# Moving scale matmuls, casts and weight loads around the start of the first token mixer (one core)

## The chip, the cores and the metric

The kernel runs on one core of a Trainium2 chip. The metric is device time in microseconds (us) of one execution; lower is better. TensorE (PE in the profile) multiplies, VectorE (DVE), ScalarE (ACT) and GpSimd (POOL) work element by element, and SyncE (SP) and GpSimd issue the transfers between HBM and the on-chip memory. Every engine runs its own instructions in order and waits for others by semaphores.

## The reference

Four layers in a row on one array x of 2048 tokens by 640 channels: a spectral layer, a token mixer, the spectral layer again, the token mixer again. Each starts from a layer norm and adds its result to x.

```python
def _A_ref(x, w_r, w_i):                      # spectral: 2-D FFT, times a filter, back
    X = jnp.fft.rfft2(x, axes=(-2, -1)) * (w_r + 1j * w_i)
    return jnp.fft.irfft2(X, s=(S, D), axes=(-2, -1))

def _B_ref(x, w1, b1, w2, b2):                # mixer over the tokens
    h = _layernorm(x, axis=-1)                                  # (B, S, D)
    u = _gelu(jnp.einsum("bsd,sf->bdf", h, w1) + b1)            # (B, D, F), F = 1728
    y = jnp.einsum("bdf,fs->bds", u, w2) + b2
    return y.transpose(0, 2, 1)

x = x + _A_ref(_layernorm(x, axis=-1), A_w_r, A_w_i)
x = x + _B_ref(_layernorm(x, axis=-1), B_w1, B_b1, B_w2, B_b2)
x = x + _A_ref(_layernorm(x, axis=-1), A_w_r, A_w_i)
x = x + _B_ref(_layernorm(x, axis=-1), B_w1, B_b1, B_w2, B_b2)
```

## The kernel before, in words

**Rows and tiles.** The 2048 tokens are 16 rows (j = 0 to 15) of 128 tokens; F is 14 tiles of 128. All products are made of float16 pairs: a value is a high part (`hi`, a cast on ScalarE) and a low part (`lo`, the rest, on VectorE), and `mm3` adds high x high, high x low and low x high in PSUM.

**Order.** While `self.pin` is set, every instruction issued through `V`, `G`, `T` or `PE` keeps its place in the program's order *on its own engine* (an edge to the instruction before it on that engine). Everything else, DMA issues among it, is placed by a planner: as soon as its operands and its buffer are free in the planner's own estimate of time, the earlier one in the program first. `with self.after(x):` puts an edge of issue order between `x` and those instructions of the block that stand on the engine of `x`.

**The stages around the change.** The first spectral layer ends in `a2(0)`, a software pipeline over the rows: step i makes the last inverse products of row i (`id_mm`), of row i - 1 (`is1_mm`), adds the result of row i - 2 to x, takes the mean and variance of row i - 3, and normalizes row i - 4 or i - 5. For that a power on GpSimd gives the factor `r`, GpSimd gives the bias `nb`, and ScalarE writes the normalized row `hf[k]`. Rows 0 to 7 get their high part `hha` right there. Between the rows stand pieces of the first weight tiles: `wload(m)` issues the two 512 KB loads `raw` of weight tile m, `scan1(m)` sums its squares on ScalarE (written to `junk`), `wsplit(m)` makes the pair `wh`, `wl` of it.

`b1st` is the first token mixer. At its start ScalarE casts rows 8 to 15 to `hhb`; `hlow(c)` makes the low parts on VectorE (`hl` for rows 0 to 7, c = 0 and 1; `hlb` for rows 8 to 15, c = 2 and 3). `prod` then multiplies them with weight tiles 0 and 1 (rows 0 to 11 first: `early`, rows 12 to 15 after: `late`), `both` with tiles 2 and 3. `keep5` forms sums of raw tiles for later use (`X`, on GpSimd) and stores them.

**Scales.** Each weight tile, or pair of tiles, has a power-of-two scale from the sum of its squares. `scale1` is a generator in three steps: the first `next` adds the sums on VectorE (`sqb`), the second is one TensorE matmul with ones (`ps<-sqb,ones`) that adds over the partitions, the third reads it on VectorE and makes the scale. `step(m)` is one `next`.

**The 35 products.** F tiles 0 to 4 and 7 to 11 are done by the seven-product scheme of Strassen and Winograd, `ops`, n = 0 to 34: `product(n)` is 24 matmuls on TensorE (eight j of `mm3`), `work(n)` the rest: `evict(n - 1)` of the PSUM result, `hi(n + 3)` and `lo(n + 3)` of a coming weight, and what `todo[n]` lists. `mms` says after which n the matmul of a scale stands:

```python
        mms = {7 * d - 6: 2 * d + PAIR for d in range(1, 5)}     # n = 1, 8, 15, 22
        mms.update({27: a, 33: b})
...
        for n in range(len(ops)):
            product(n)
            work(n, todo[n])
            if n in mms:
                step(mms[n])
```

The first step of that scale is in `todo[n]`, the third in `todo[n + 1]`. After the 35 products come the 16 rows of the second product (the loop over j, 28 entries i of up to three matmuls each), which also starts the next spectral layer; it is not pinned up to j = 12. There the last two steps of the scale of tile m + 2 stand at i = 6 and 7.

The second mixer, `b2nd`, begins with the same casts of rows 8 to 15, but not pinned.

Of the kernel before, what the change touches and what calls it, by code (L numbers as in the profile page):

```python
# [15 lines left out]
AF = mybir.ActivationFunctionType  # L16
ALU = mybir.AluOpType
# [3 lines left out]
S, D, NL, F = 2048, 640, 321, 1728  # L21
NJ, NG, NFT = 16, 16, 14
# [32 lines left out]
PAIR = 4  # L55
# [35 lines left out]
class Layers:  # L91
# [697 lines left out]
    def a2(self, li):  # L789
        nc, A = self.nc, self.A  # L790
        first = li == 0
        V, G, T = self.V, self.G, self.T
# [11 lines left out]
        p = self.push("a2", side=self.sq)  # L804
# [50 lines left out]
        xt, pd, eo, p1, ec, mv, vs, rb = ({} for _ in range(8))  # L855
# [3 lines left out]
        for i in range(NJ + 5):  # L859
            has = [0 <= i - k < NJ for k in range(6)]  # L860
            if has[0]:
                pd[i] = id_mm(i)
            if has[1]:
                k = i - 1
                eh, ps = eo[k], pd.pop(k)
                el = elow(ps, eh)
                if not first and i == NJ:
                    self.pss0 = self.big()
                    for j in HA:
                        for a in range(2):  # L870
                            mm(self.pss0[:, a, :320], self.w[0][0][:, j], self.hh[j][:, a], start=j == 0, stop=False)
                p1[k] = is1_mm(eo.pop(k), el, tIM[k // 4][:, k % 4])
            if first and i == 10:
                next(sc)
            if has[4]:
                v, mean = vs.pop(i - 4)
                r = self.t(p, [128, 1], F32, "r", 3)
                G.tensor_tensor(r, v, self.mh, op=ALU.pow)
                b = self.t(p, [128, 1], F32, "nb", 3)
                G.tensor_scalar(b, mean, r, -1.0, op0=ALU.mult, op1=ALU.mult)  # L880
                rb[i - 4] = r, b
            if has[2]:
                k = i - 2
                x, ps = xt[k], p1.pop(k)
                o = ps[:, 1]
                e = self.t(p, [128, 324], F32, "ec", 2)
                T.activation(e[:, :322], ps[:, 0, :322], AF.Copy)
                V.tensor_tensor(v2(x, 160, NL), v2(x, 160, NL), v2(o, 161, 1), op=ALU.subtract)
                V.tensor_tensor(x[:, :NL], x[:, :NL], o[:, :NL], op=ALU.add)
                if first and i == 11:  # L890
                    next(sc)
                G.tensor_tensor(v2(x, 160, NL), v2(x, 160, NL), v2(e, 161, 1), op=ALU.add)
                G.tensor_tensor(x[:, :NL], x[:, :NL], e[:, :NL], op=ALU.add)
            for k in (i - 4,) if not first or i >= NJ else (i - 5,) if i < NJ - 1 else (i - 5, i - 4):
                if not 0 <= k < NJ:
                    continue
                r, b = rb.pop(k)
                f = self.hf[k]
                T.activation(f, xt.pop(k)[:, :D].rearrange("p (a b) -> p a b", a=2), AF.Identity, scale=r, bias=b)
                if k in HA:  # L900
                    T.activation(self.hh[k], f, AF.Copy)
            k = i if first else i + 1
            if 2 <= k < NJ:
                xt[k] = xload(k)
            if has[2]:
                nc.sync.dma_start(self.xs[li + 1][i - 2], xt[i - 2][:, :D])
            if has[3]:
                st = self.stats1(p, xt[i - 3])
                m = self.stats2(p, st)
                v = self.t(p, [128, 1], F32, "v", 2)  # L910
                V.tensor_scalar(v, m[:, 1:2], (1.0 + EPS) / ZS ** 2, EPS * EPS / ZS ** 2, op0=ALU.mult, op1=ALU.add)
                vs[i - 3] = v, m[:, 0:1]
            if has[0]:
                eo[i] = ehigh(pd[i])
            if i in (1, 2):
                self.wsplit(0, (1,), hi=False, part=slice(i * 4 - 4, i * 4))
            if first and i in (4, 5):
                self.wsplit(0, (0,), hi=False, part=slice(i * 4 - 16, i * 4 - 12))
            if i == 3:
                self.wload(1)  # L920
                self.wopen(1)
            if first:
                if i in (6, 7):
                    self.scan1(1, (i - 6,))
                if i == 8:
                    sc = self.scale1(1, at=lambda: p1[i - 1][:, 1, 400:401])
                    next(sc)
            if i in (12, 13):
                self.wsplit(1, (i - 12,), lo=False)
            if first and i == 14:  # L930
                self.wsplit(1, (0,), hi=False)
            if first and i in (10, 13, 16):
                self.wload({10: 2, 13: 3, 16: 5}[i])
            if i in (1, 4, 8):
                mload()
        self.pin = False
# [116 lines left out]
    def b1st(self, li):  # L1053
        nc, A = self.nc, self.A
        V, G, T = self.V, self.G, self.T
# [6 lines left out]
        H = self.halves(ph, pt, hx)  # L1062
        prod, tsum, thi, tlo, hlow, hhigh, hlows = H.prod, H.tsum, H.thi, H.tlo, H.hlow, H.hhigh, H.hlows
        spot = [None]
        sc = {m: self.scale1(m, at=lambda m=m: spot[0][:, m % 4:m % 4 + 1]) for m in range(2, NFT + 2)}
        sc.update({m: self.scale1(m) for m in range(NFT + 2, NFT + NJ)})
        self.pin = True

        def step(m):
            if m in sc:  # L1070
                next(sc[m])
# [17 lines left out]
        def keep5(a):  # L1089
            ssum(5, a, G)  # L1090
            nc.gpsimd.dma_start(self.ws1[5][a], src(5, a))
# [19 lines left out]
        bank, f = {}, {}  # L1111

        def product(n):
            o = self.big()
            bank[n], spot[0] = o[:, 0, :320], o[:, 1, 0:4]
            for j in range(8):
                self.mm3(bank[n], (wo[n][:, 0, j], wo[n][:, 1, j]), H.operand(PB[ops[n][1]], j), j == 0, j == 7)

        def gelu(o, x=None, **q):
# [56 lines left out]
        upart = lambda ft, a, i: U[ft % 7][:, i, ft // 7 * 2 + a]  # L1176


        for j in range(8, NJ):
            T.activation(H.hhb[:, j - 8], self.hf[j], AF.Copy)  # L1180
        self.wsplit(1, (1,), hi=False)
        self.wload(PAIR)
        self.scan1(2)
        self.scan1(3)
        hlow(0)
# [10 lines left out]
        hlow(2)  # L1196
        step(2)
        step(3)
        keep5("S1")
        prod(pss[1], w1[0], hhigh, early, start=True)  # L1200
        step(3)
        self.scan1(4)
        self.scan1(5)
        hlow(3)
        step(3)
        step(4)
        for i, q in ((0, w0[0]), (0, w0[1]), (1, w1[0])):
# [56 lines left out]
        for d in range(1, 5):  # L1264
            a, b, n = 2 * d + PAIR, 2 * d + PAIR + 1, 7 * d
# [10 lines left out]
        a, b = NFT, NFT + 1  # L1276
# [10 lines left out]
        todo[32] += [lam(self.wopen, a), lam(self.wsplit, a, (0,))]  # L1287
        todo[33] += [lam(self.wsplit, a, (1,))]
        todo[34] += [lam(uhi, 4, 0, 2), lam(ulo, 4, 0, 2)]
        mms = {7 * d - 6: 2 * d + PAIR for d in range(1, 5)}  # L1290
        mms.update({27: a, 33: b})

        for e in todo[-5]:
            e()
        for j in every:
            if j % 4 == 0:
                work(j // 4 - 4, todo[j // 4 - 4])
            both(ps, w, j)
            if j % 4 == 3 and j // 4 - 4 in mms:
                step(mms[j // 4 - 4])  # L1300
        plain(3, f[5][:, 2:4], flat(ps))
        for n in range(len(ops)):
            if n == 3:
                self.pop("hf")
                pu = self.push("u", side=self.sp)
                U.update({e: pu.tile([128, 2, 4, 320], F16, name=f"u{e}_{self.n}") for e in range(7)})
            product(n)
            work(n, todo[n])
            if n in mms:
                step(mms[n])  # L1310
        evict(len(ops) - 1)
        evicted(len(ops) - 1)
        uhi(4, 2, 2)
# [11 lines left out]
        p = self.pT  # L1325
# [42 lines left out]
        for j in range(NJ):  # L1368
# [7 lines left out]
            xt = xts[j][:, :D]  # L1376
# [17 lines left out]
            for i, (ft, a) in enumerate(order):  # L1394
                if tail and i == NFT:
                    half(0)
                if j == NJ - 2 and i in (4, 20):
                    flush(1)
                if j >= NJ - 2 and i in (6, 12, 17):
                    next(row)  # L1400
                if tail and i == 2:
                    self.wopen(0)
                    self.wsplit(0, lo=False)
                if i in (4, 8):
                    next(steps, None)
                if j == NJ - 3 and i == 9:
                    self.wload(0)
                if i in (6, 7):
                    step(m + 2)
                if i in (15, 18):  # L1410
                    self.scan1(m + 3, (i // 3 - 5,))
                if i == 26 and m + 3 < NFT + NJ:
                    step(m + 3)
                o = pss[a][:, :320]
                if ft < NFT - 1:
                    self.mm3(o, (wh[:, ft], wl[:, ft]), (upart(ft, a, 0), upart(ft, a, 1)), ft == SEQ[0], ft == SEQ[-1])
                else:
                    mm(o, wh[:, ft], upart(ft, a, 1), start=False, stop=False)
                    mm(o, wl[:, ft], upart(ft, a, 0), start=False, stop=False)
# [722 lines left out]
```

## Time and profile before

| | |
|---|---|
| Time, median of 3 runs | 998.46 us (997.73 to 999.18) |
| The profiled execution | 1002.54 us; its span, first to last instruction, 1000.5 us |
| Mean granted TensorE clock over the span | 0.986 |
| PE busy | 942.2 us (94%), 9009 matmuls |
| DVE, ACT, POOL busy | 758.1 us (76%), 563.8 us (56%), 325.9 us (33%) |
| Moved by DMA | 176.28 MB, mean 176 GB/s |

All times below are us from the start of the span. In the profile's lines nearly all instructions have line 83, which is the helper that issues them, so they are told apart by the names of their tiles: `out<-in`. `a2(0)` lies at about 122 to 179, the start of `b1st` at 179 to 229, the 35 products at 237 to 360, the rows of the second product from there to about 555. The same places of the second half of the kernel lie at 622 to 678 and from there on. A row of the timeline gives start, duration, engine, instruction, tiles, count, and in brackets the idle time of the engine before it with what ended it. A row of the windows gives the stretch, its length, the busy time of PE, weight loads, DVE, ACT, POOL with counts, the granted clock (1.00 is full speed), the share of time in which the DMA engines were busy, and GB/s.

### The profile page before, as it was taken

What the parts mean: (1) busy time and instruction counts of PE and PEld (TensorE: products, weight loads), DVE (VectorE), ACT (ScalarE), POOL (GpSimd) and SP (SyncE); (2) the same over time, 40 slices, a digit from 0 to 9 for tenths busy, and PEclk for the clock granted to TensorE, in tenths of its full rate; (3) what the DMA queues carried; (4) which work ended last, traced back from release to release, by engine and by line L of the source; (5) the groups of instructions that cost most, each with busy time, mean ns of one, the idle gap of its engine ahead of it and who ended that gap; (6) DMA issues with size and microseconds to landing.
All of it is one profiled execution on the core that took longest, in us unless ns stands there. A gap on an engine that the chain in (4) does not pass through costs nothing.

```text
span 1000.5 us, 22481 instructions
## 1 busy us (share of the span) xinstructions
PE 942.2 (94%) x9009; PEld 697.2 (70%) x9009; DVE 758.1 (76%) x1392; ACT 563.8 (56%) x864; POOL 325.9 (33%) x515
## 2 busy tenths in 40 slices
PE   4889898699999989999999998999999999999998
PEld 3768776376677657777777687776777777777776
DVE  7989878879877866666666798789834455998885
ACT  5857768757656667555543377585533444454431
POOL 6949757551222322222222298573000000000000
PEclk9999999799999999999999999999999999999999
DMA  8866386345777675464321465475555447755411
GB/s 260 274 176 172 118 308 231 122 138 182 246 248 247 212 251 183 134 207 129 125 86 73 138 186 168 148 230 170 183 154 167 144 131 247 242 170 198 146 46 53
DMA packets 67244, 176.28 MB, mean 176 GB/s; under 512 B 7914, under 2 KB 15236, under 8 KB 67140
## 3 DMA queue, kind: packets, MB, share of 16 engines
q1 hardware_dynamic: 59380, 146.39, 46.6%
q0 software_dynamic: 7760, 28.46, 7.6%
q8 instruction: 70, 1.15, 0.5%
q14 instruction: 34, 0.28, 0.1%
HBM read 127.24 MB, written 47.58 MB: 175 GB/s over the span
## 4 chain that ended last, share of the span: by engine, by line
PE 50%; DVE 7%; ACT 3%; POOL 3%; issue 2%; DMA 2%; SPq 0%; DVEq 0%; ACTq 0%; POOLq 0%
PE ps L83 50%; DMA raw<-w2z 1%; DVE xt L83 1%; DVE u L83 1%; DVE wl L83 1%; POOL ta L83 1%; POOL xl L83 1%; DVE st L83 1%; DVE S L83 1%; POOL xt L83 1%; ACT eh L83 1%; DMA w<-w 0%; DVE wh L83 0%; DMA stk<-rest 0%; ACT xh L83 0%
## 5 line engine op out<-in xcount | busy, mean ns | idle before, releaser
L83 PEld LDWEIGHTS <-wh 128*128 128x128 f16 x2298 | 223.2, 98 | 99.5 <-issue 11.6
L83 PE MATMUL ps<-u,wh 128*128 128x320 f16 x1242 | 233.3, 300 | 0.2 <-DVE wh L83 0.2
L83 PEld LDWEIGHTS <-wl 128*128 128x128 f16 x1626 | 160.4, 99 | 70.2 <-issue 6.1
L83 PE MATMUL ps<-u,wl 128*128 128x320 f16 x826 | 186.8, 300 | 0.0
L83 PEld LDWEIGHTS <-wo 128*128 128x128 f16 x924 | 90.3, 98 | 37.2 <-issue 2.1
L83 POOL TENSOR_TENSOR r<-v,mh 128x1 f32<-128x1 f32 x64 | 37.7, 588 | 144.1 <-DVE nm L83 134.3
L83 PE MATMUL ps<-tDi,Yh 128*128 128x322 f16 x320 | 72.7, 305 | 1.0 <-ACT Yh L83 1.0
L83 DVE TENSOR_TENSOR f<-eo 128x256 f32<-128x256 f32 (+1 forms) x124 | 39.6, 372 | 36.5 <-POOL eo L83 36.0
L83 POOL TENSOR_TENSOR xt<-xt,ec 128x320 f32<-128x320 f32 x64 | 53.3, 854 | 34.7 <-DVE xt L83 34.6
L83 ACT ACTIVATE junk<-raw 128x896 bf16<-128x896 f32 (+1 forms) x60 | 59.4, 990 | 4.9 <-DMA raw<-w 4.5
L83 DVE BATCH_NORM_STATS2 st<-xt 128x6 f32<-128x320 f32 x126 | 55.3, 481 | 5.0 <-DMA xt<-x 4.4
L83 PE MATMUL ps<-u,wo 128*128 128x320 f16 x420 | 58.8, 299 | 0.0
L83 POOL TENSOR_TENSOR eo<-z 128x320 f32<-128x320 f32 x60 | 52.4, 894 | 17.4 <-ACT z L83 15.7
L83 PE MATMUL ps<-tDi,Yl 128*128 128x322 f16 x192 | 56.6, 303 | 1.4 <-DVE Yl L83 1.4
L83 PE MATMUL ps<-tM,f 128*128 128x128 f32 x160 | 39.2, 417 | 19.4 <-DVE f L83 19.3
L83 DVE SCALAR_TENSOR_TENSOR wl<-raw,s,wh 128x896 f16<-128x896 f32 (+2 forms) x43 | 48.7, 1138 | 11.0 <-ACT wh L83 10.8
L83 ACT ACTIVATE z<-xt,nb,r 128x640 f32<-128x640 f32 x31 | 28.5, 918 | 46.8 <-POOL z L83 38.3
L83 PE MATMUL ps<-hhb,wh 128*128 128x320 f16 x224 | 46.0, 304 | 8.3 <-ACT hhb L83 8.2
L83 PEld LDWEIGHTS ps<-tM,f 128*128 128x128 f32 x160 | 33.1, 297 | 25.4 <-DVE f L83 25.0
L83 ACT ACTIVATE wh<-raw,s 128x896 f16<-128x896 f32 (+2 forms) x46 | 43.5, 988 | 9.1 <-PE ps L83 7.6
L83 POOL MEMSET wl<- 64x256 f16 x2 | 0.6, 307 | 146.6 <-DMA wl<-w2A 146.6
L83 POOL TENSOR_TENSOR xl<-ta,xh 128x642 f16<-128x642 f32 (+2 forms) x34 | 45.5, 1346 | 5.9 <-ACT xh L83 5.9
(263 smaller groups left out, 2349.0 us busy)
## 6 DMA issues: line engine op xcount, KB each, us to landing
xt<-x SPq DMA_DIRECT2D x79, 320.0 KB
raw<-w SPq DMA_DIRECT2D x32, 512.0 KB
w<-w SPq DMA_DIRECT2D x48, 321.0 KB
x<-xt SPq DMA_DIRECT2D x47, 320.0 KB
raw<-w SPq DMA_DIRECT2D x32, 448.0 KB
raw<-w2z SPq DMA_DIRECT2D x32, 448.0 KB
out<-xt SPq DMA_DIRECT2D x15, 320.0 KB
tIM<-tIM POOLq DMA_DIRECT2D x8, 512.0 KB, 4.9
```

What stands on the lines that cost most here:

```text
L83: i = f(*a, **k)
```

## The change

Six edits, all in the first half of the kernel:

1. `a2(0)`, i = 19: the bias `nb` of the last row is made on VectorE instead of GpSimd.
2. `a2(0)`: the loads of weight tiles 2 and 3 stand at i = 15 and 17 instead of 10 and 13, inside `self.after(pace)`, where `pace` is the ScalarE normalization last issued. The load of tile 5 moves from i = 16 to the start of `b1st`.
3. The low part of the second half of tile 1 (`wsplit(1, (1,), hi=False)`) moves from the start of `b1st` to i = 18 of `a2(0)`.
4. The eight casts `hhb` move ahead of `self.pin = True`: they are no longer pinned.
5. `keep5("S1")` is written after `hlow(3)` instead of before the products of tile 1.
6. The scale's matmul moves from behind `work(n)` into `product(n + 1)`, after 15 of its 24 matmuls; in the second product's row j = 0 its last two steps move from i = 6 and 7 to i = 18 and 19.

```diff
@@ a2 @@
-                G.tensor_scalar(b, mean, r, -1.0, op0=ALU.mult, op1=ALU.mult)
+                (V if first and i == NJ + 3 else G).tensor_scalar(b, mean, r, -1.0, op0=ALU.mult, op1=ALU.mult)
...
-                T.activation(f, xt.pop(k)[:, :D].rearrange("p (a b) -> p a b", a=2), AF.Identity, scale=r, bias=b)
+                pace = T.activation(f, xt.pop(k)[:, :D].rearrange("p (a b) -> p a b", a=2), AF.Identity, scale=r, bias=b)
...
-            if first and i in (10, 13, 16):
-                self.wload({10: 2, 13: 3, 16: 5}[i])
+            if first and i in (15, 17):
+                with self.after(pace):
+                    self.wload(i // 2 - 5)
+            if first and i == 18:
+                self.wsplit(1, (1,), hi=False)
@@ b1st @@
+        for j in range(8, NJ):
+            T.activation(H.hhb[:, j - 8], self.hf[j], AF.Copy)
         self.pin = True
...
             for j in range(8):
+                if j == 5 and n in mms:
+                    step(mms[n])
                 self.mm3(bank[n], (wo[n][:, 0, j], wo[n][:, 1, j]), H.operand(PB[ops[n][1]], j), j == 0, j == 7)
...
-        for j in range(8, NJ):
-            T.activation(H.hhb[:, j - 8], self.hf[j], AF.Copy)
-        self.wsplit(1, (1,), hi=False)
         self.wload(PAIR)
+        self.wload(PAIR + 1)
...
-        keep5("S1")
         prod(pss[1], w1[0], hhigh, early, start=True)
         step(3)
         self.scan1(4)
         self.scan1(5)
         hlow(3)
+        keep5("S1")
...
-        mms = {7 * d - 6: 2 * d + PAIR for d in range(1, 5)}
-        mms.update({27: a, 33: b})
+        mms = {7 * d - 5: 2 * d + PAIR for d in range(1, 5)}
+        mms.update({28: a, 34: b})
...
-            if n in mms:
-                step(mms[n])
...
-                if i in (6, 7):
+                if i in ((6, 7) if j else (18, 19)):
                     step(m + 2)
```

More of the change, by code (lines that the diff above doesn't have):

```diff
@@ L1298, in b1st @@
             both(ps, w, j)
-            if j % 4 == 3 and j // 4 - 4 in mms:
-                step(mms[j // 4 - 4])
         plain(3, f[5][:, 2:4], flat(ps))
```

## The prediction

> **What bounds the kernel now.** The page's busy times come first, then the list of waits of TensorE, because an engine that is busy 94% of the span gains only where it stands still or runs at a lower clock.
>
> ```profile
> PE 942.2 (94%) x9009; PEld 697.2 (70%) x9009; DVE 758.1 (76%) x1392; ACT 563.8 (56%) x864; POOL 325.9 (33%) x515
> ```
> ```profile
> PE ps L83 <- DVE f L83: 19.3, 19, 11.3
> PE ps L83 <- DVE sqb L83: 9.0, 4, 3.3
> PE ps L83 <- ACT hhb L83: 8.2, 3, 7.9
> PE ps L83 <- DVE el L83: 4.3, 6, 1.2
> ```
>
> The first wait is the start of the kernel, which the change leaves alone. The other three are what the six edits touch: the scale matmuls (9.0 us in four waits), the casts of rows 8 to 15 (8.2, nearly all in one wait), and low parts in `a2` (4.3 over both halves). The timeline of TensorE shows where they stand.
>
> ```profile
> 178.71 2.35 PE L83 MATMUL ps<-hha,wh 128*128 128x320 f16 x16
> 188.91 2.57 PE L83 MATMUL ps<-hhb,wh 128*128 128x320 f16 x8 [7.85 <-ACT hhb L83]
> 196.10 0.17 PE L83 MATMUL ps<-sqb,ones 128*128 128x1 bf16 x1
> 199.51 0.16 PE L83 MATMUL ps<-sqb,ones 128*128 128x1 bf16 x1
> ...
> 246.22 0.16 PE L83 MATMUL ps<-sqb,ones 128*128 128x1 bf16 x1 [1.94 <-DVE sqb L83]
> 271.65 0.16 PE L83 MATMUL ps<-sqb,ones 128*128 128x1 bf16 x1 [2.44 <-DVE sqb L83]
> 276.61 0.30 PE L83 MATMUL ps<-hhb,wh 128*128 128x320 f16 x1
> 336.89 0.16 PE L83 MATMUL ps<-sqb,ones 128*128 128x1 bf16 x1 [1.39 <-DVE sqb L83]
> 359.76 0.43 PE L83 MATMUL ps<-u,wh 128*128 128x320 f16 x2
> 367.27 0.16 PE L83 MATMUL ps<-sqb,ones 128*128 128x1 bf16 x1 [3.27 <-DVE sqb L83]
> ```
>
> Sixteen matmuls in 2.35 us, the last lasting 0.30, start (2.35 - 0.30) / 15 = 0.137 us apart; I use 0.136 for one and 3.27 for a product of 24. A wait also costs clock. In the windows, the granted clock is 0.50 behind each of the longer waits:
>
> ```profile
> 188.90:194.40 5.50, 5.49 (x20) 2.77 (x20) 3.29 (x1) 5.47 (x10) 2.58 (x2) 0.50 0.23 95
> 229.60:268.10 38.50, 36.56 (x271) 26.22 (x269) 38.18 (x40) 26.81 (x35) 8.31 (x12) 1.00 0.55 195
> 269.50:272.90 3.40, 1.25 (x10) 0.90 (x10) 1.35 (x2) 1.76 (x3) 0.53 (x1) 1.00 0.94 270
> 272.90:276.40 3.50, 3.50 (x16) 2.03 (x14) 2.12 (x7) 2.60 (x4) 0.53 (x1) 0.51 0.99 290
> 320.80:367.10 46.30, 41.81 (x309) 29.88 (x307) 41.21 (x65) 31.01 (x40) 14.04 (x16) 1.00 0.68 230
> 368.60:371.90 3.30, 3.30 (x14) 1.84 (x13) 0.35 (x3) 2.66 (x6) 0.00 (x0) 0.50 0.93 284
> ```
>
> A stretch of 3.4 us in which PE was busy for 1.25 is followed by one of 3.4 at half clock: 1.7 us of work lost on top of the wait. The waits of 1.94 and 1.39 brought none.
>
> **Edits 1 to 5, the start of `b1st`.** These rows are the last row's path; the second half of the kernel, where the casts already stand outside the fixed order, follows them.
>
> ```profile
> 183.85 0.98 POOL L83 TENSOR_TENSOR r<-v,mh 128x1 f32<-128x1 f32 x1 [0.57 <-DVE v L83]
> 184.93 2.35 POOL L83 TENSOR_SCALAR nb<-mv,r 128x1 f32<-128x1 f32 x1
> 187.24 3.60 POOL L83 TENSOR_TENSOR X<-raw,raw 128x1024 f32<-128x1024 f32 x1
> ...
> 188.14 5.11 ACT L83 ACTIVATE hhb<-hf 128x640 f16<-128x640 f32 x8
> ...
> 184.34 7.85 DVE L83 TENSOR_TENSOR hl<-hf,hha 128x1280 f16<-128x1280 f32 x4
> 195.50 0.16 DVE L83 TENSOR_REDUCE sqb<-sqFalse 128x1 bf16<-128x2 f32 x1 [3.31 <-ACT junk L83]
> 195.57 2.82 DVE L83 TENSOR_TENSOR hlb<-hf,hhb 128x2560 f16<-128x2560 f32 x1
> 199.31 0.15 DVE L83 TENSOR_REDUCE sqb<-sqFalse 128x1 bf16<-128x2 f32 x1
> ```
> ```profile
> 678.09 1.97 ACT L83 ACTIVATE hhb<-hf 128x640 f16<-128x640 f32 x3
> 680.42 0.89 DVE L83 TENSOR_TENSOR xt<-xt,ps 128x320 f32<-128x320 f32 x2 [1.27 <-ACT ec L83]
> 685.22 5.69 DVE L83 TENSOR_TENSOR hl<-hf,hha 128x1280 f16<-128x1280 f32 x4
> ```
>
> Edit 4: with casts between the rows, as at 678.09 (their cover is ACT's waiting for the next bias; where it is gone, see the `ec` below), rows 8 to 11 are ready when PE has done its first 16 matmuls, and PE runs on. It does 48 matmuls from 178.71 and reaches the scale matmul of tile 2 at 178.71 + 48 x 0.136 = 185.3. The wait is then for that matmul's sum (`sqb`), which stands on DVE behind the last row's `nb` and the four subtractions `hl`. Edit 1 puts `nb` there: it waits for `r` (184.83) and should take about 0.15, as the one-column sum at 199.31 does, so `hl` starts at about 185.05 instead of 184.34. If the casts also push back the `ec` of row 15, as the 1.27 us at 680.42 show, it is about 186.1. The four subtractions took 7.85 us beside the POOL sum `X` and 5.69 without it, so `X` costs them 2.16. Edit 5 doesn't take `X` away: nothing else stands on POOL's queue after `r`, and being written later in the program holds nothing back there, so `X` will run right after `r`. `hl` then ends at 192.9 to 194.0, and the scale matmul stands at 193.1 to 194.2 instead of 196.10: 1.9 to 3.0 us gained of a wait of 7.85.
>
> Then the clock: PE has stood idle for 8 us and starts at half clock. Before, the slow matmuls (188.91 to 194.4) lay ahead of a time that DVE set anyway; now they lie behind it. I take the mean of a half window that remains and, in two cases of three, another one: 4.1 us, 2.05 of it lost (0 to 3.3). The next scale matmul comes 24 matmuls later, 193.1 to 194.2 + 3.27 + 2.05 = 198.4 to 199.5, against 199.51. DVE would allow it a little earlier (2.82 for `hlb`, 0.92 from its end to the sum at 199.31, 0.15 for that sum). Edit 3 leaves DVE's order as it is. Sum of this part: a gain of 0 to 1.1; I take **0.6**. Ends: if all eight casts (5.11) came ahead of the last row, -4.5; if `X` ran elsewhere and the clock stayed full, the chain on DVE ends 4.5 earlier than now, +4.5.
>
> Edit 2, the loads:
>
> ```profile
> 23.73 0.43 SPq L337 DMA_DIRECT2D tD<-tD  x1
> ...
> 24.86 0.18 POOL L83 COPY eo<-z 128x2 f32<-128x2 f32 x1
> ...
> 103.34 1.63 SPq L958 DMA_DIRECT2D raw<-w  x2
> 138.82 0.43 SPq L958 DMA_DIRECT2D raw<-w  x1
> ```
>
> Six loads written for i = 10 to 16 (by `a2`'s 122 to 179 for its steps, about 150 and later: an estimate) were issued from 103.34 on, the last by 138.82: the planner issues them when buffer and queue are free, wherever they are written. The edge of `self.after` binds instructions of `pace`'s own engine, ScalarE, and the loads stand on SP. The same form with a POOL instruction held nothing before: the table load at 23.73 left ahead of that POOL copy of row 5 (24.86). So I count **0**, for the loads of tile 5 too. Ends: 0 and the 4.3 of the `el` waits, if x rows land sooner; a loss is a rival below.
>
> **Edit 6 at 246.22 and 271.65.** Each matmul moves 15 matmuls, 2.04 us, later. At 246.22 the whole 1.94 goes. But DVE is busy 38.18 of 38.5 us before 268.1, so its sums don't come earlier because PE does: PE comes to the next one at 271.65 - 2.44 - 1.94 + 2.04 = 269.31 and waits 2.3 us inside the product. What is left of it is then 9 matmuls, so it ends at 271.8 + 1.2 = 273.0 instead of 276.6, a gain of 3.6. A wait of 2.3 that falls anywhere in the windows of 3.4 fills about half of one of them in three cases of four, which costs 1.7: on average 1.3. The waits of the next two scales were nothing; they may cost 0.1. Sum: **2.2** (ends 0 and 1.94 + 2.44 + 1.7 = 6.1). The third step stays in `work(n + 1)` on DVE, which comes to it after the matmul's new place.
>
> *By a page:* the Trainium skill ("TensorE: Matmul & The Clock Gate", Part 1) has the clock fall after at least one whole idle window of 3.4 us. The 0.51 behind a window with 1.25 us of work contradicts this; by the page's rule the 1.3 would not be subtracted and the part would be 3.5.
>
> **Edit 6 at 336.89 and 367.27.** DVE is busy 41.21 of 46.3 us here, and the chain that ended last runs over DVE and ACT, past the wait at 336.89:
>
> ```profile
> 335.94 1.25 ACT u L83
> 337.19 1.05 ACT wl L83
> ...
> 367.06 0.17 DVE sqb L83
> 367.27 32.77 PE ps L83 x239
> ```
>
> So the sum at 367.06 comes no earlier. The 1.39 goes, and PE comes to the second product's rows at 359.76 - 1.39 = 358.4; at i = 18 it has 54 matmuls behind it, 365.7, and waits 1.5 us instead of 3.27. It leaves at 367.3 as before, but with 54 matmuls done instead of 30: 24 x 0.136 = 3.27, plus the 1.7 of the half window at 368.6, less 0.5 for the cases in which 1.5 us bring one. Sum: **4.5** (ends 3.3 and 1.39 + 3.27 + 1.7 = 6.4). Behind it DVE takes PE's result late, since the x rows land at their old time; the other PSUM buffers cover that.
>
> **The sum.** 0.6 + 0 + 2.2 + 4.5 = 7.3 us. The profiled execution took 1002.54 us (span 1000.5), 4.1 above the median; it would become 995.2, and the median 998.46 - 7.3 = 991.2.
>
> **Rivals.**
> 1. *The loads are held back after all.* Then x rows meet less traffic in `a2`; half of the 4.3 gives 2.1 more: 989. For it: the 4.3. Against it: the rows at 23.73 and 24.86. Chance 0.15.
> 2. *The sum `X` keeps clear of the subtractions*, as the new place of `keep5` reads, and the shorter wait keeps the clock: the upper end named above, 3.9 more, 987.3. Against it: `X` followed `nb` at once, though written after `hlow(2)`. Chance 0.13.
> 3. *DVE, ACT or transfers stay the bound through both stretches of edit 6*: PE's lead is taken back at the next evictions and loads (DMA share 0.94 to 0.99 at 269.5 to 276.4), and of 6.7 only 2 are left: 995.9. Chance 0.10.
> 4. *Casts in front.* All eight delay the last row, the end named above: -4.5 + 6.7 = 2.2, 996.3, hardly a change. Chance 0.07.
> 5. *Slower: held loads land last.* If tile 3's loads wait for row 13 and its neighbours' traffic, eight loads of 0.5 MB and four rows of 0.32 MB, 5.5 MB at the page's mean of 176 GB/s, are 31 us: from 176 to 207. Two squares-sums follow at 1.2 us each, and the scale matmul stands at 209.7 instead of 199.51: 10.2 lost, 6.7 gained, 1002. It decides from a landing at 204 on. Against it: the queues moved 290 GB/s in the window at 272.9. Chance 0.04.
>
> **How the numbers follow.** My forecast has 0.51 (988 to 994 us). The measurement of this kernel can tell about 0.2%, 2.0 us, so "same" is 996.5 to 1000.5. Faster: 0.51 + 0.15 + 0.13 + 0.06 of the third + 0.03 of the fourth = 0.88; same: the rest of these two, 0.08; slower 0.04. The range 984.5 to 996.5 takes in both ends of the first part and rivals 1 and 2, and leaves out about 0.15.
>
> **What the next profile would show.** Right: casts `hhb` between the rows' `hf` before 188; no wait for `hhb` but one of 7 to 9 us at the scale matmul after 48 matmuls, with clock 0.50 behind it; `nb` on DVE at 0.15 to 0.2; `X` right behind `r`, and `hl` at 7 to 8 us for four; the raw loads again from 103 on; of the scale waits none at 246, about 2.3 us near 270, about 1.5 near 366. Wrong: `raw` issued after 175, `X` after `hl`, new waits for evictions or `raw` between 250 and 320, or a last row's `hf` later than 188.23.

## The result and the profile after

The changed kernel takes 989.6 us (median of 4 runs, 987.3 to 990.5) against 998.1 for the kernel before: ratio 0.9914, 95% interval 0.989 to 0.9939, so 8.5 us less. Forecast were 991.2 and a gain of 7.3.

The profiled execution took 989.35 us, the one before 1002.54. That is 13.2 apart, more than the medians, so the two traces can't be subtracted as they stand. They can be laid on each other: apart from the 26 scale matmuls, both kernels do the same 8983 matmuls in the same order, and each has a start time in both traces. The lead of the changed kernel grows as follows (positions of the kernel before; the last two rows are not part of the change):

| stretch | lead gained, us | what ended there |
|---|---|---|
| last row's `el` (177.9) to the second scale matmul (199.5) | 0.67 | edits 1 to 5 |
| 246 | 2.04 | wait of 1.94 |
| 272 to 277 | 1.67 | half clock behind the wait of 2.44; the wait itself stays |
| 336 to 372 | 4.20 | waits of 1.39 and 3.27, half clock; less two waits of 0.81 and 1.31 |
| before 177.9 | 3.24 | waits for `xl` and `el`, a half-clock window; no changed instruction |
| after 560 | 1.20 | half-clock windows; no changed instruction |

The four stretches of the change give 8.58 us, about the difference of the medians. The 1.67 among them is chance: TensorE waits 2.44 us in both traces, and only in the first did half clock follow. The rest is two executions of the same work with other waits.

The list of TensorE's waits after (us in total, times, longest): the wait for `hhb` is down from 8.2 to 0.4, and `sqb` is up from 9.0 to 11.2, in three waits instead of four.

```profile
PE ps L83 <- DVE sqb L83: 11.2, 3, 7.4
...
PE ps L83 <- DVE el L83: 3.0, 5, 1.0
...
PE ps L83 <- ACT hhb L83: 0.4, 2, 0.2
```

The timeline of TensorE after (start, us, operation, and in brackets the idle time ahead of it and who ended it): 48 matmuls without a stop, then one wait of 7.43; no wait at 242.30 and 329.76, where 246.22 and 336.89 stood; 2.44 again at 267.75, and 1.31 at 360.12. New is 0.81 at 352.52.

```profile
175.47 2.35 PE L83 MATMUL ps<-hha,wh 128*128 128x320 f16 x16
177.66 1.25 PE L83 MATMUL ps<-hhb,wh 128*128 128x320 f16 x8
...
189.59 0.19 PE L83 MATMUL ps<-sqb,ones 128*128 128x1 bf16 x1 [7.43 <-DVE sqb L83]
189.64 4.43 PE L83 MATMUL ps<-hha,wh 128*128 128x320 f16 x16
...
195.60 0.17 PE L83 MATMUL ps<-sqb,ones 128*128 128x1 bf16 x1
...
242.30 0.16 PE L83 MATMUL ps<-sqb,ones 128*128 128x1 bf16 x1
...
267.75 0.16 PE L83 MATMUL ps<-sqb,ones 128*128 128x1 bf16 x1 [2.44 <-DVE sqb L83]
...
329.76 0.17 PE L83 MATMUL ps<-sqb,ones 128*128 128x1 bf16 x1
...
352.52 0.31 PE L83 MATMUL ps<-u,wl 128*128 128x320 f16 x1 [0.81 <-DVE wl L83]
...
360.12 0.16 PE L83 MATMUL ps<-sqb,ones 128*128 128x1 bf16 x1 [1.31 <-DVE sqb L83]
```

The other engines around the last row, after: a cast stands behind a row's `hf`, `X` directly behind `r`, and the four `hl` take 7.71.

```profile
180.62 0.98 POOL L83 TENSOR_TENSOR r<-v,mh 128x1 f32<-128x1 f32 x1 [0.57 <-DVE v L83]
181.57 2.35 POOL L83 TENSOR_TENSOR X<-raw,raw 128x1024 f32<-128x1024 f32 x1
...
181.63 0.21 DVE L83 TENSOR_SCALAR nb<-mv,r 128x1 f32<-128x1 f32 x1 [0.44 <-POOL r L83]
181.76 7.71 DVE L83 TENSOR_TENSOR hl<-hf,hha 128x1280 f16<-128x1280 f32 x4
...
193.19 0.15 DVE L83 TENSOR_REDUCE sqb<-sqFalse 128x1 bf16<-128x2 f32 x1
...
181.03 0.74 ACT L83 ACTIVATE hhb<-hf 128x640 f16<-128x640 f32 x1
181.88 0.92 ACT L83 ACTIVATE hf<-xt,nb,r 128x640 f32<-128x640 f32 x1
```

And the windows after (PE busy, PEld, DVE, ACT, POOL, granted clock, DMA share, GB/s): half clock from the idle stretch until 195.1, so that 24 matmuls take 6 us instead of 3.3.

```profile
185.00:189.50 4.50, 0.00 (x0) 0.00 (x0) 4.50 (x6) 4.38 (x9) 0.00 (x0) 0.50 0.28 117
189.60:195.10 5.50, 5.50 (x22) 3.17 (x23) 5.33 (x9) 3.21 (x6) 0.00 (x0) 0.50 0.00 0
195.20:203.20 8.00, 8.00 (x61) 5.79 (x60) 3.23 (x10) 0.00 (x0) 0.00 (x0) 1.00 0.01 2
```

### The profile page after: what moved, and what is told of

The parts are those of the page before. It is cut to its first block, busy times and chain, and to the rows that moved or that the text cites. A ratio compares the mean times of both kernels' runs of the same rounds, so it can differ in the third digit from the quotient of the medians.

```text
span 987.5 us, 22475 instructions
## 1 busy us (share of the span) xinstructions
PE 936.8 (95%) x9009; PEld 694.8 (70%) x9009; DVE 755.6 (77%) x1393; ACT 563.1 (57%) x864; POOL 321.4 (33%) x514
## 4 chain that ended last, share of the span: by engine, by line
PE 61%; DVE 19%; issue 5%; ACT 5%; POOL 5%; DMA 4%; SPq 1%; DVEq 0%; ACTq 0%; POOLq 0%
PE ps L83 61%; DVE f L83 2%; DVE st L83 2%; DVE xt L83 1%; DVE wl L83 1%; DVE Yl L83 1%; DMA raw<-w2z 1%; DVE s1l L83 1%; POOL xt L83 1%; DVE wh L83 1%; DVE u L83 1%; POOL xl L83 1%; POOL ta L83 1%; DMA raw<-w 1%; DVE hl L83 1%
## 5 line engine op out<-in xcount | busy, mean ns | idle before, releaser
L83 PE MATMUL ps<-tM,f 128*128 128x128 f32 x160 | 40.3, 433 | 18.8 <-DMA xt<-x 11.5
```

Source lines behind the costliest of these rows:

```text
L83: i = f(*a, **k)
```

## The experiments

All ratios are to the kernel before, timed beside it (997.3 to 998.3 us); the changed kernel's is 0.9914. "Aligned" positions are the start of the same matmul counted from the last row's last matmul (at 175.33 in the changed kernel), against the changed kernel's trace, so that what happened earlier drops out. The heads of the columns are places on the changed kernel's clock. A minus is earlier.

| kernel | low parts, 205 | ahead of 268 | behind it, 272 | in the second product, 363 | ratio |
|---|---|---|---|---|---|
| before | +0.67 | +2.71 | +4.38 | +8.58 | 1 |
| edits 1 to 5 | +0.01 | +3.73 | +2.05 | +6.27 | 0.9989 |
| edit 6 | +0.73 | +0.72 | +0.71 | +0.72 | 0.9932 |
| edit 6, products | +0.88 | +0.89 | +0.88 | +2.52 | 0.9965 |
| edit 2 undone | -1.36 | -1.36 | +0.31 | +0.32 | 0.9914 |
| edit 4 undone | -1.55 | -1.54 | +0.04 | +0.05 | 0.9911 |
| loads held | -2.03 | -2.03 | -2.04 | -2.03 | 0.9878 |
| `X` behind `hl` | -2.42 | -2.42 | -2.43 | -2.42 | 0.9887 |
| scale matmul late | -4.71 | -4.76 | -3.14 | -3.13 | 0.9895 |
| late, `X` behind `hlb` | -8.05 | -6.69 | -5.02 | -5.01 | 0.9861 |
| sums first | -0.24 | -0.29 | -2.88 | -2.87 | 0.9887 |
| all together | -7.90 | -7.08 | -9.18 | -10.66 | 0.9789 |

Each row is a single trace, the ratio is of many runs. A stretch of 3.41 us at half clock costs 1.7, and the trace of the kernel before has two of them in the products and behind (from 272.97 and from 368.54), and that of the changed kernel none, so a difference of 1.7 in one column need not be the edit's.

**Edit 6 alone**, on the kernel before (both halves of its diff).

> The kernel before with edit 6 alone: the scale matmuls of the products inside the next product, and those of the second product at i = 18 and 19. Theory: the parts of the gain add up as the two traces show them matmul by matmul, 3.4 us at the two waits of 246 and 271 and 4.5 at those of 337 and 367, so 7.9 us under the kernel before, ratio 0.992. Rival A: the gain came from the first row of the new b1st, whose scale matmul stands 6.5 us earlier; then edit 6 alone gives 2 us or less, ratio 0.998 to 1. Rival B: the 3.2 us by which the changed kernel was ahead before any changed instruction belong to the change; then this kernel, in which nothing ahead of 240 is changed, shows no lead there.

Measured: 990.86 us, 0.9932 [0.9917, 0.9947], 6.8 us. The bulk of the gain is here. Its trace stands 0.7 behind the changed kernel from the start of `b1st` on and does not move again up to 547: what edits 1 to 5 leave is that 0.7. As for rival B, at 149 its trace is level with the changed kernel's (148.84 and 149.36 for the same `el` matmul, 151.35 before), with none of the edits ahead of 240; the lead ahead of the change was no part of it.

**Edits 1 to 5 alone.**

> The changed kernel with edit 6 undone, so edits 1 to 5 alone. Theory: the scale matmul of tile 2 stands 3 us earlier, and the granted clock takes that back behind the wait; the next scale matmul is 0.7 us earlier, 0.7 us under the kernel before, ratio 0.999. Rival A: the 6.5 us of the first scale matmul are kept, 992 us, ratio 0.9935. Rival B: the casts between the rows delay the rows and it is slower, by up to 1 us.

Measured: 995.78 us, 0.9989 [0.9977, 1.0], some 1.1 us. The interval reaches to nothing. The first scale matmul stands 3.3 us earlier, counted from the last row's last matmul (14.26 us behind it against 17.54), and the clock takes all but 0.7 of that back; the 6.5 of the rival held 3.2 of lead from ahead of the change. With edit 6's 6.8 this makes 7.9 of 8.5: the two halves add.

**Edit 6 in the products alone** (`if i in (6, 7)` in the second product stays).

> The kernel before with the first half of edit 6 alone: the scale matmuls inside the products, not those of the second product's rows. Theory: the wait of 1.94 us at 246 goes, that of 2.44 near 270 stays, and what it costs in clock depends on where it falls in the windows: 2.0 us (no half window either way) to 3.7 (as between the two traces), ratio 0.9970, between 0.996 and 0.998; the rest of edit 6's 0.9932 is then the second product's. Rival: the first half is given back at ScalarE's and VectorE's next waits, and all of edit 6 lies in the second product; ratio 0.9985 to 1.0005.

Measured: 994.54 us, 0.9965 [0.9953, 0.9977], 3.5 us. The other 3.3 of edit 6, with some 2 either way by the two intervals, are the second product's. The expectation overlooked that the wait of 1.39 at 336.89 is a product's too (n = 27): this trace has none there, at 330.19. It still has 2.43 near 268, 0.82 at 352.95 and 2.95 at 360.55, 6.2 us against 9.0 in the four waits of the kernel before, so 2.8 are waits, and what the ratio has beyond that is clock or noise.

**Edit 2 undone**: the loads where they were, without the edge.

```
-            if first and i in (15, 17):
-                with self.after(pace):
-                    self.wload(i // 2 - 5)
+            if first and i in (10, 13, 16):
+                self.wload({10: 2, 13: 3, 16: 5}[i])
```

> The changed kernel with edit 2 undone: the raw loads of tiles 2, 3 and 5 are written where they stood before, without the edge. Theory: every queue of this kernel holds the same instructions in the same order as the changed kernel's, so edit 2 does nothing and this is the changed kernel run once more: ratio 0.9914, between 0.989 and 0.9935. Rival: the edge or the place decides when the loads leave; then the loads before 145 stand at other times than in the changed kernel, and the ratio moves by more than 0.002.

Measured: 989.41 us, 0.9914 [0.9899, 0.993], the changed kernel to the last digit; all five engines hold the same instructions in the same order. Edit 2 has no effect. It also shows how far two traces of one program differ: 1.4 us at the start of `b1st`, where this one ran at half clock for 6.83 us and the other for 10.24, and 1.7 us at 272, from one half-clock window.

**The loads truly held.** The edge goes to an instruction of the loads' own queue:

```
+                store = nc.sync.dma_start(self.xs[li + 1][i - 2], xt[i - 2][:, :D])
...
-                with self.after(pace):
+                with self.after(store):
                     self.wload(i // 2 - 5)
```

> The changed kernel with the loads of tiles 2 and 3 really held: the edge of edit 2 goes to the store of the x row of the same step, which stands on SP as the loads do. Theory: the loads leave some 30 us later; the waits for el in a2 depend on the row's arithmetic and hardly change, the loads still land ahead of their scans, and the time is that of the changed kernel within 1 us, ratio 0.9904 to 0.9924. Rival 1 of the prediction: x rows land sooner, 2.1 us less, ratio 0.989. Rival 5: the loads land last, ScalarE's squares of tiles 2 to 5 wait for them, and it is up to 10 us slower, ratio 1.00.

Measured: 985.45 us, 0.9878 [0.986, 0.9896]: 3.6 us under the changed kernel. My expectation fell. Rival 1's mechanism is there, with 1.6 us of the 2.1 it was priced at, and another 2.0 come from `X`. SP's timeline of this kernel has no load of weights between 140.23 and 168.95; `X` on POOL now waits for one and runs behind three of the four `hl`, which take 5.69. The fence has the rows of SP, POOL and VectorE.

```profile
168.95 0.33 SPq L961 DMA_DIRECT2D raw<-w  x1
...
172.25 0.92 SPq L961 DMA_DIRECT2D raw<-w  x2
...
184.94 2.69 POOL L83 TENSOR_TENSOR X<-raw,raw 128x1024 f32<-128x1024 f32 x1 [5.38 <-DMA raw<-w]
...
179.73 5.69 DVE L83 TENSOR_TENSOR hl<-hf,hha 128x1280 f16<-128x1280 f32 x4
185.33 0.15 DVE L83 TENSOR_REDUCE sqb<-sqFalse 128x1 bf16<-128x2 f32 x1
185.40 4.91 DVE L83 TENSOR_TENSOR hlb<-hf,hhb 128x2560 f16<-128x2560 f32 x1
```

That is 2.0 of the 3.6. The other 1.6 are in `a2`, by the two traces 1.2 at the wait for `el` at 149.36 and 0.4 up to 153. In the changed kernel VectorE waits for an x row behind ten us in which the DMA engines are 95% busy, and TensorE then waits for `el`; with the loads held the share is 0.76 and both waits are gone. TensorE's wait here is 0.75 to 1.54 us in all eleven traces in which the loads are not held, and none in the two in which they are. The timeline of the changed kernel first, then its window from 135 to 145, then the same window of this one:

```profile
146.39 0.89 DVE L83 TENSOR_TENSOR xt<-xt,ps 128x320 f32<-128x320 f32 x2 [2.19 <-DMA xt<-x]
...
149.36 0.41 PE L83 MATMUL ps<-el,tIM 128*128 128x322 f32 x1 [1.05 <-DVE el L83]
```
```profile
135.00:145.00 10.00, 10.00 (x73) 7.72 (x72) 8.99 (x22) 8.53 (x13) 8.26 (x13) 1.00 0.95 322
```
```profile
135.00:145.00 10.00, 10.00 (x73) 7.84 (x72) 9.79 (x24) 8.90 (x14) 8.48 (x14) 1.00 0.76 245
```

**Edit 4 undone**: the casts behind the last row again (the loop moved back ahead of `self.wload(PAIR)`).

> The changed kernel with edit 4 undone: the casts of rows 8 to 15 stand behind the last row again. Theory: PE waits for them some 6 us after 16 matmuls and does the next 32 at half clock, but now ahead of the sum that VectorE and ScalarE give at about 9.8 us behind r; the scale matmul of tile 3 then stands 13.7 to 15 us behind r, against 14.98 in the changed kernel, so moving the casts is worth nothing by itself: ratio 0.9904 to 0.9919. Rival: the casts carry the gain at the start; without them that scale matmul stands where it stood in the kernel before (15.66 behind r) or later, ratio 0.992 to 0.994.

Measured: 988.94 us, 0.9911 [0.9895, 0.9927]. The casts' new place is worth nothing. TensorE's timeline of this kernel shows why: it waits 5.64 for `hhb` instead of 7.43 for `sqb`, does its slow matmuls there, and both scale matmuls then wait only for VectorE (0.16 and 0.34). Edit 4 exchanges one wait for another.

```profile
184.45 2.57 PE L83 MATMUL ps<-hhb,wh 128*128 128x320 f16 x8 [5.64 <-ACT hhb L83]
...
191.25 0.18 PE L83 MATMUL ps<-sqb,ones 128*128 128x1 bf16 x1 [0.16 <-DVE sqb L83]
...
195.05 0.16 PE L83 MATMUL ps<-sqb,ones 128*128 128x1 bf16 x1 [0.34 <-DVE sqb L83]
```

**`X` behind `hl`**, by a POOL copy that reads the last `hl`:

```
         hlow(3)
+        G.tensor_copy(self.t(self.base, [128, 1], F16, "hold", 1), H.hl1[:, 7, 319:320])
         keep5("S1")
```

> The changed kernel, with the POOL sum X put behind a POOL copy of one column that reads the last of the four subtractions hl, so that X truly runs after them. Theory: hl takes 5.9 us instead of 7.7 and the scale matmul of tile 2 stands 1.8 us earlier, but X now lies beside the subtraction hlb (2.8 us), which takes 4.8, and the next scale's sum stands where it stood: within 0.3 us of the changed kernel, ratio 0.991 to the kernel before. Rival 2 of the prediction: 3.9 us under the changed kernel, ratio 0.9875, because DVE's chain is shorter and PE keeps its clock.

Measured: 987.08 us, 0.9887 [0.9869, 0.9905], 2.7 under the changed kernel: between my 0.3 and the rival's 3.9. `hl` took 5.69 as both said. Two things were wrong in mine. In the changed kernel the second scale matmul was not held by its sum (ready at 193.34, above) but by TensorE's own half clock (195.60), so an earlier restart counts in full. And `X` did not fall beside the first `hlb`: the copy of one column took 2.78 us, to the end of that `hlb`, and `X` then cost the second one 1.2.

```profile
183.55 5.69 DVE L83 TENSOR_TENSOR hl<-hf,hha 128x1280 f16<-128x1280 f32 x4
...
189.22 2.81 DVE L83 TENSOR_TENSOR hlb<-hf,hhb 128x2560 f16<-128x2560 f32 x1
...
193.02 4.05 DVE L83 TENSOR_TENSOR hlb<-hf,hhb 128x2560 f16<-128x2560 f32 x1
...
189.30 2.78 POOL L83 COPY hold<-hl 128x1 f16<-128x1 f16 x1 [5.92 <-DVE sqb L83]
192.04 2.35 POOL L83 TENSOR_TENSOR X<-raw,raw 128x1024 f32<-128x1024 f32 x1
```

**The scale matmul of tile 2 behind all high parts**, that of tile 3 behind 24 matmuls on low parts:

```
         prod(pss[0], w0[1], hhigh, early)
+        prod(pss[1], w1[0], hhigh, early, start=True)
+        for i, q in ((0, w0[0]), (0, w0[1]), (1, w1[0])):
+            prod(pss[i], q, hhigh, late)
         step(2)
...
-        prod(pss[1], w1[0], hhigh, early, start=True)
+        prod(pss[0], w0[0], hlows, range(12))
         step(3)
```

> The changed kernel with the scale matmul of tile 2 put behind all 96 matmuls on high parts (48 before) and that of tile 3 behind 24 matmuls on low parts. Theory: PE needs 96 x 0.136 = 13.1 us from 175.5, comes to the scale matmul at 188.7 and waits 1 us instead of 7.4, at full clock; the low parts end at about 198 instead of 203.2, set by hlb, and the weights of tile 2, whose buffer PE then frees, follow 5 us earlier, since ScalarE stood idle for 10.6 us and VectorE for 6.0 before them: 5 us under the changed kernel, ratio 0.986 to the kernel before. Rival: VectorE, busy nearly all the time up to 268, takes the lead back at the next waits: within 1 us of the changed kernel, ratio 0.991.

Measured: 988.03 us, 0.9895 [0.9879, 0.9911], 1.9 under the changed kernel, between the two expectations. The scale matmul of tile 2 waits 0.90, at full clock, as the theory has it, and the low parts are 4.7 earlier, which it put at 5. But TensorE now waits 2.55 for the second `hlb`, at 198.17, and 3.41 us of half clock lie over that wait and behind it, from 197.52. Behind 265 the lead is 3.1: the wait of 2.4 there brought a half-clock window in this trace and none in the changed kernel's. The 1.2 that the ratio lacks beside that are within its interval.

**Both of these**, with `X` behind the second `hlb` (the copy reads `H.hlb[:, 7, 1, 319:320]`).

> The kernel with the scale matmul of tile 2 behind all high parts, and the POOL sum X behind a copy of one column that reads the last subtraction hlb. Theory: both shortened the same stretch, by 2.4 (X) and 4.7 us (order) at the scale matmul of tile 4, matmul against matmul; together PE waits only for the second hlb and the scale matmul stands 7.0 to 7.5 us earlier than in the changed kernel, measured from the last row. X, beside other VectorE work later, costs up to 2 there. Ratio 0.985, between 0.983 and 0.988. Rival: VectorE takes the second part back at its next sums; ratio 0.9895 as with the order alone.

Measured: 984.35 us, 0.9861 [0.9845, 0.9876], 5.3 under the changed kernel. The scale matmul of tile 4 stands 8.05 earlier, more than expected; then 1.26 is lost at a scale matmul near 235 that VectorE now gives late, and 1.7 to a half-clock window at 261.8.

**The sums first**, ahead of their product's other VectorE work:

```
-            for k in (6, 5):
-                todo[n - k].append(lam(step, a))
+            first[n - 6] = a
+            todo[n - 5].append(lam(step, a))
...
             product(n)
+            step(first.get(n))
             work(n, todo[n])
```

> The changed kernel with the sums of the products' scales (sqb) put ahead of the other VectorE work of their product instead of behind it. Theory: the 2.44 us at the scale matmul near 268 are not VectorE's load, as the prediction had it, but its order: the sum stands behind a low part (wl) that waits 2.19 us for ScalarE, while its own squares are done at 264.9. The wait goes, and with it 2.4 us, 4.1 where it brought a half window; ratio 0.9885, between 0.987 and 0.990. Rival: VectorE is the bound here, as the 38.18 of 38.5 us say; PE then waits as long for the next evictions, and the ratio stays at 0.9914.

Measured: 986.65 us, 0.9887 [0.987, 0.9905], 2.7 under the changed kernel; the wait is gone and nothing takes its place up to 349. VectorE's timeline of the changed kernel, and then of this one, shows the order at work:

```profile
266.34 1.28 DVE L83 SCALAR_TENSOR_TENSOR wl<-raw,sp,wl 128x1024 f16<-128x1024 f32 x1 [2.19 <-ACT wl L83]
267.54 0.15 DVE L83 TENSOR_REDUCE sqb<-sqTrue 128x1 bf16<-128x4 f32 x1
```
```profile
264.47 0.16 DVE L83 TENSOR_REDUCE sqb<-sqTrue 128x1 bf16<-128x4 f32 x1 [0.74 <-ACT junk L83]
265.92 1.29 DVE L83 SCALAR_TENSOR_TENSOR wl<-raw,sp,wl 128x1024 f16<-128x1024 f32 x1 [1.29 <-ACT wl L83]
```

**All together**: loads held, both at the start, sums first, and `(22, 23)` for `(18, 19)` in the second product's first row.

> The changed kernel with the loads held by SP's own store, the scale matmul of tile 2 behind all high parts, X behind hlb, the sums of the products' scales first, and the scale matmul of the second product's first row at i = 23. Theory: the parts lie in different stretches and add, counted against the changed kernel: 1.2 (el wait in a2), 4.8 (start of b1st), 2.9 to 4.2 (sum near 268), 1.3 (i = 23); 10.2 to 11.5 us, ratio 0.981, between 0.979 and 0.983. Rival: VectorE or ScalarE, nearly full up to 268, give back what lies ahead of them, and the best of the parts alone is hardly beaten: ratio 0.985 to 0.986.

Measured: 976.85 us, 0.9789 [0.977, 0.9807]: 20.7 us under the kernel before and 12.5 under the changed one, against the 10.2 to 11.5 expected; 0.9789 lies just below the range that was given from 0.979. The parts with runs of their own gave 3.6, 5.3 and 2.7; that of the second product's first row has none, and in this trace its scale matmul has no wait left (1.31 in the changed kernel). In its list of waits no line for `sqb` is left among the ten longest; TensorE is busy 96% of the span (page), and at the start of `b1st` it waits 2.27 for the second `hlb` (timeline).

```profile
PE 929.8 (96%) x9009; PEld 690.0 (71%) x9009; DVE 756.2 (78%) x1393; ACT 562.5 (58%) x864; POOL 322.4 (33%) x515
```
```profile
186.01 0.17 PE L83 MATMUL ps<-sqb,ones 128*128 128x1 bf16 x1
189.29 0.17 PE L83 MATMUL ps<-sqb,ones 128*128 128x1 bf16 x1
191.73 1.25 PE L83 MATMUL ps<-hlb,wh 128*128 128x320 f16 x8 [2.27 <-DVE hlb L83]
```

## Why the prediction was right, and where not

*The start of `b1st` (forecast 0.6, aligned traces 0.67, edits 1 to 5 alone 1.1).* Casts in the gaps, no wait for `hhb`, a wait of 7.43 (7 to 9 said), `nb` 0.21, `X` right behind `r`, `hl` 7.71 (7.85 assumed). Counted from `r`'s start, the first scale matmul came after 8.97 us and the second after 14.98, on the old trace's clock 192.8 and 198.8, against 193.1 to 194.2 and 198.4 to 199.5. The first is 0.3 earlier than the lower end: `hl` started 1.14 behind `r`'s start (1.20 assumed) and ran 0.14 shorter; the `ec` of row 15 was not pushed back. The half clock cost 2.8 (5.6 us of half clock with TensorE at work), not 2.05, and that more than took the 0.3 back; the second scale matmul still came within the range. The casts themselves, which the prediction gave as the way to the gain, are worth nothing. No run takes edits 1, 3 and 5 apart, so which of them holds the 0.7 is open.

*The loads (0).* Right, and for the reason given: the edge on ScalarE's instruction does not bind SP's queue.

*The scale matmuls at 246 and 271 (2.2; aligned 3.7).* The wait that stays was forecast as 2.3 and is 2.44. The term that was mis-sized is the half window. The forecast's 3.6 holds the whole 1.7 of the one in the trace before, as if it came each time, and takes off 1.3 for one after the change. The same wait stands on both sides, and of ten traces with it five had the window (below), so 0.85 belongs on each side, and the two cancel. Of the aligned 3.7, 2.04 are the wait at 246 and 1.67 the window that the changed kernel's trace happened not to have; an estimate of the part's mean is then about 2.0, and that the 2.2 is so near it is in part luck.

One reason was wrong though the number held: the sum was not held by a saturated VectorE. The window of 38.18 busy of 38.5 us ended at 268.1, just where VectorE begins to stand for ScalarE's `wl`. VectorE's timeline before has the row:

```profile
270.25 1.28 DVE L83 SCALAR_TENSOR_TENSOR wl<-raw,sp,wl 128x1024 f16<-128x1024 f32 x1 [2.19 <-ACT wl L83]
271.45 0.15 DVE L83 TENSOR_REDUCE sqb<-sqTrue 128x1 bf16<-128x4 f32 x1
```

A busy share up to the wait was taken for the cause of the wait, and it hid a gain of 2.7.

*The scale matmuls at 337 and 367 (4.5; aligned 4.2).* The waits were forecast as none and 1.5, and are none and 1.31. In the aligned positions 1.57 is won at 336, 1.0 lost at 352 and 3.64 won at 367; 1.7 of the last are the half window at 368.54, which the forecast counted too. By the ratios, the one at 367 brought 3.3, some 2 either way, and the one at 337 is in the 3.5 of the products. The loss is the new wait of 0.81 for `wl` at 352.52, which the prediction did not have: TensorE comes sooner, and the low part of the weights does not.

*The rivals.* Loads held (1) did not happen; had they been, it would have been 3.6 and not 2.1, since the held load also keeps `X` away; the x rows alone are worth 1.6. `X` clear (2) did not happen and is worth 2.7, not 3.9: the clock does not stay full. Neither VectorE's bound (3) nor casts in front (4) showed. The slower case (5), held loads landing last, is refuted: held, they landed in time.

*The clock.* The rule of the Trainium skill ("TensorE: Matmul & The Clock Gate", Part 1) that the prediction weighed, that the clock falls after at least one whole idle window, is contradicted again: 1.95 us idle in a window of 3.41 was enough. The last section has the rows.

## What to carry to other kernels

Where two engines wait on each other's order, ask of each wait what its releaser stood behind in its queue just then, and not how busy that engine was on average: the sum near 268 was 0.2 us of work behind someone else's wait. Look whether an ordering edge lies on the queue of the instruction that it is meant to hold; the loads here were held only by an instruction of their own queue, and that was worth more than what the change brought at the start. And lay traces on each other matmul by matmul before subtracting them: of 13.2 us between these two profiles, 4.4 had nothing to do with the change, and 1.7 more were a half-clock window that the same wait brought in one trace and not in the other.

## What the hardware showed that was not expected

*The clock's windows.* Nearly the same wait, of 2.39 to 2.44 us, stands near 265 in ten of the traces. TensorE's clock changes in a grid of 3.41 us, the same through the run: in the trace before, half clock begins at 115.96, 184.22, 272.97 and 368.54, which are 20, 26 and 28 windows apart. In five traces the wait put 2.10 to 2.39 us of idle time into one window, and the next window ran at half clock; in five it was split over two, with at most 1.77 in one, and the clock stayed full. A wait of 1.95 that lay whole in one window (edits 1 to 5, at 241) brought a half window too, and 1.85 us idle (edit 6, products, from 358.7) brought none. So between 240 and 370 the limit lies between about 1.85 and 1.95 us idle in a window of 3.41, a half window costs 1.7 us of work, and whether a wait of 2.4 us brings one depends on where it falls in the grid, which is chance. It is no limit for the whole kernel: in other stages, with other matmuls (near 52, 112 and 600), windows with 1.39 to 1.80 us idle were followed by half clock in some cases and not in others, and what decides there is not shown. The windows of the kernel with edit 2 undone, with 1.11 us of work ahead of the drop, and then two of the changed kernel, a drop behind 1.53 us idle:

```profile
263.30:266.60 3.30, 1.11 (x10) 0.80 (x9) 2.42 (x3) 3.24 (x4) 0.53 (x1) 1.00 0.95 273
266.70:270.00 3.30, 3.30 (x14) 1.84 (x13) 2.87 (x10) 2.25 (x3) 0.53 (x1) 0.50 0.95 253
```
```profile
51.82:55.23 3.41, 1.88 (x12) 1.30 (x11) 3.38 (x9) 2.78 (x7) 2.37 (x6) 1.00 0.51 131
55.24:58.65 3.41, 3.35 (x15) 3.35 (x16) 3.34 (x11) 1.24 (x3) 0.00 (x0) 0.50 0.74 252
```

*POOL and VectorE.* A POOL copy of one column that met a running `hlb` took 2.78 us and ended with it (192.08 and 192.03), and an `hlb` that met a running `X` ended 2.68 us after `X` did, about its own 2.82. So in these cases they don't slow each other in proportion; the second waits for the first. The Trainium skill ("SBUF — State Buffer", section "SBUF: two separate sides") says the same of a VectorE operation with two SBUF inputs and a GpSimd operation that reads SBUF: an exclusive lock, held for the whole instruction. The traces agree.
